# Sliding-window attention and a feed-forward layer on one core: group 1's last additions between the value rows of batch 2, its last block transposed on TensorE, and batch 4's loads and casts ahead of the row scalings of batch 3

## The chip, the cores and the metric

The kernel runs on one core of a Trainium2 chip. The metric is the device time of one execution in microseconds (us). Before the change the median of three runs is 306.37 us (306.21 to 306.56).

## What is computed

Attention with 8 batches, 8 heads, 576 positions and 64 values per head; a position sees itself and the 63 before it. Its output, with the heads side by side, is the input x of a normalised two-layer feed-forward block with a residual:

```
scores = q @ k^T / 8            # masked to 0 <= i - j < 64
attn   = softmax(scores)
x      = attn @ v               # 8 x 576 x 512
xn     = (x - mean) / sqrt(var + 1e-6) * g_ln
out    = x + relu(xn @ w_ch1) @ w_ch2      # 512 -> 2048 -> 512
```

## The kernel before

**Groups.** The first 512 positions of batch g are group g (0 to 7); the last 64 positions of all batches make group 8. While TensorE (PE) runs the feed-forward products of group g, the same loop iteration also runs the attention of batch g+1 in between, and loads and casts batch g+2. A block is 128 of a group's 512 rows, so a group has blocks 0 to 3; "(2,3)" below is batch 2, block 3.

**Units and slots.** The products of a group are a list of 30 units (`mlp_units`). In groups 1 and 2, units 0 to 7 are the first layer for blocks 0 and 1, units 8 to 15 the first layer for blocks 2 and 3 (`l1_half`, L639, tile hph, 8 matmuls each, evacuated with a ReLU by ScalarE (ACT), L644, into hrT). Two PSUM banks ("mm") take turns, so unit n+2 waits for the evacuation of unit n. Units 16 to 29 are the second layer as seven half-size products (L572, banks pA, pB, pC); their operands are sums that VectorE (DVE) makes of hrT (`s_sums`, L546) and of the second weights (`w2_sums`, L833). DVE adds each finished bank into x (`post`, L585; `post_both`, L581), and the rows are stored (L533). Group 3 and later use full-width first-layer units (L498, tile hps), whose first unit reads all four blocks of zT.

Everything else is put between the units by hand: `at(i, f, ...)` appends a step to slot i, which is issued after unit i; slot 30 is after the last unit. Within a slot, steps go in the order in which they were appended. Each engine and each DMA queue works its instructions in that order; waits come from the data and from buffers that are used again.

**The steps of a block.** `s_pe` (L349): scores on PE, into the banks "sc", "xps" or the two banks t0 and t1 ("t"). `s_exp` (L359): two exponentials on ACT. `s_mask` (L369): one multiplication on DVE. `b_pe` (L396): the product with v. `b_rows`: on DVE reciprocal and scaling by rows into x_norm (L412, L416), then mean and variance (L418, L421). `z_step`: three small operations on POOL (GpSimd; L440 to L442, tile rsz), and from batch 3 on the normalised block z there too (L446); for batches 1 and 2 z is made apart, by `z_act` (ACT, L452), `z_dve` (DVE, L461) or `z_pool` (POOL, L457). `zt_step`: transposes z into zT, for batches 0 and 1 by four PE transposes (L475) and a copy by ACT (L478) or DVE (L480), from batch 2 on by a DMA transpose on SP's queue (L471), apart from block 3 of batches 3 and 5.

**The steps of a batch.** `load_qk(b, half)` (L92) and `load_v` (L176): loads on SP's queue; a half is four heads. `cast_qk` (L154) and `cast_v` (L182): POOL. `t_main(b, x, half)`: transposes q (x = 0) or k (x = 1) of four heads into qkT, for batch 2 on PE (L276) with a copy by ACT (L257) or DVE (L259); from batch 3 on q goes by a DMA transpose (L265). `part_vB` (L201, L203): copies by DMA. `load_tail`, `cast_tail`, `t_tail` (L104 to L106, L116 to L118, L298, L307): the same for two batches' rows of group 8. qkT of batch b is the buffer of batch b-2. z has three buffers, so z of (3,3) takes that of (3,0). A PE transpose in group 2 takes bank t0 or t1.

The steps of group 1 are at L1010 to L1074; those of group 2 at L1075 to L1080, the shared part L1081 to L1126, and L1134 to L1152.

Of the kernel before, what the change touches and what calls it, by code (L numbers as in the profile page):

```python
# [10 lines left out]
FP32 = mybir.dt.float32  # L11
FP16 = mybir.dt.float16
AF = mybir.ActivationFunctionType
ALU = mybir.AluOpType
# [4 lines left out]
def kernel(  # L19
# [10 lines left out]
    nc = tc.nc  # L30
    B, H, S, D = q.shape
# [3 lines left out]
    NGRP = B + 1  # L35
# [5 lines left out]
    XZ = 2  # L41
# [9 lines left out]
    p_blk = ctx.enter_context(tc.tile_pool(name="pblk", bufs=3))  # L51
# [28 lines left out]
    x_norm, zT, mvg, zsd, rstd = {}, {}, {}, {}, {}  # L80
# [316 lines left out]
                                 rhs=rhs, start=True, stop=True)  # L397

    def b_rows(g, kb):
        kblk = f"{g}_{kb}"  # L400
        sfx, nb = ("r", 2) if g == NGRP - 1 else ("", None)
        if kb % 2 == 0:
            if (g, kb // 2) not in x_norm:
                for h in ((1, 0) if g // 2 == 2 else (0, 1)):
                    x_norm[(g, h)] = p_xn.tile([128, 2, DM], FP32, tag="xn" + sfx, name=f"xn_{g}_{h}", bufs=nb)
        xv = x_norm[(g, kb // 2)][:, kb % 2, :]
        xn = xv.rearrange("p (h d) -> p h d", h=H)
        tiles = xpss.pop((g, kb))
        n = H // len(tiles)
        rcp = p_blk.tile([128, H], FP32, tag="rcp", name=f"rcp_{kblk}")  # L410
        for i, xps in enumerate(tiles):
            nc.vector.reciprocal(out=rcp[:, n * i:n * i + n], in_=xps[:, :, D])  # L412
        for i, xps in enumerate(tiles):
            rc = rcp[:, n * i:n * i + n]
            rcp_b = bass.AP(tensor=rc.tensor, offset=rc.offset, ap=[rc.ap[0], rc.ap[1], [0, D]])
            nc.vector.tensor_tensor(out=xn[:, n * i:n * i + n], in0=xps[:, :, 0:D], in1=rcp_b, op=ALU.mult)  # L416
        stats = p_blk.tile([128, nc.vector.BN_STATS_DIM], FP32, tag="stats", name=f"stats_{kblk}")
        nc.vector.bn_stats(out=stats, in_=xv)  # L418
        if g not in mvg:
            mvg[g] = p_grp.tile([128, 4, 2], FP32, tag="mvg" + sfx, name=f"mvg_{g}", bufs=1 if sfx else 2)  # L420
        nc.vector.bn_aggr(out=mvg[g][:, kb, :], in_=stats)  # L421
        if g == 0 and kb != 2:
            z_step(g, kb)
# [24 lines left out]
    rsnm = {}  # L448
# [3 lines left out]
        nc.scalar.activation(out=zsd[(g, kb)], in_=x_norm[(g, kb // 2)][:, kb % 2, :], func=AF.Identity,  # L452
                             bias=nm, scale=rs)

    def z_pool(g, kb):
        rs, nm = rsnm[(g, kb)]
        nc.gpsimd.tensor_scalar(out=zsd[(g, kb)], in0=x_norm[(g, kb // 2)][:, kb % 2, :], scalar1=rs, scalar2=nm,  # L457
                                op0=ALU.mult, op1=ALU.add)

    def z_dve(g, kb):  # L460
        nc.vector.tensor_scalar(out=zsd[(g, kb)], in0=x_norm[(g, kb // 2)][:, kb % 2, :],  # L461
                                scalar1=mvg[g][:, kb, 0:1], scalar2=rsnm[(g, kb)][0],
# [2 lines left out]
    def zt_step(g, kb, eng="act"):  # L465
        z = zsd.pop((g, kb))
        if g not in zT:
            sfx = "r" if g == NGRP - 1 else ""
            zT[g] = p_grp.tile([128, NKC, 512], FP16, tag="zT" + sfx, name=f"zT_{g}", bufs=1 if sfx else 2)
        if XZ <= g and not (kb == 3 and g in (3, 5)):  # L470
            nc.sync.dma_start_transpose(out=zT[g][:, :, 128 * kb:128 * kb + 128], in_=z)  # L471
            return
        ztp = t_tile([128, NKC, 128], f"ztp_{g}_{kb}")
        for kc in range(NKC):
            nc.tensor.transpose(out=ztp[:, kc, :], in_=z[:, 128 * kc:128 * (kc + 1)], identity=ident16)  # L475
        dst = zT[g][:, :, 128 * kb:128 * kb + 128]
        if eng == "act":
            nc.scalar.copy(out=dst, in_=ztp)  # L478
        else:
            nc.vector.tensor_copy(out=dst, in_=ztp)  # L480
# [362 lines left out]
    for i in range(8):  # L843
# [8 lines left out]
        out=mask[0:64], in_=mask[0:64], compare_op=ALU.is_gt, fill=0.0,  # L852
# [3 lines left out]
        out=mask[64:128], in_=mask[64:128], compare_op=ALU.is_ge, fill=0.0,  # L856
# [87 lines left out]
    for g in range(NGRP):  # L944
# [7 lines left out]
        def at(i, f, *a):  # L952
            slots[min(i, len(slots) - 1)].append((f, a))

        def first_scores(b, i):
            at(i, s_pe, b, 0)
            at(i, s_pe, b, 1, False, "xps")
            at(i, s_exp, b, 0, 0, 1)
            at(i + 1, s_exp, b, 1, 0, 1)
            at(i + 1, s_mask, b, 0)  # L960
            at(i + 2, s_mask, b, 1)

        b = g + 1
# [46 lines left out]
        if g == 1:  # L1010
            at(0, cast_qk, 2, 0, (0,))
            at(0, after_mask, 1, 3)
            at(0, cast_qk, 2, 0, (1,))
            at(0, cast_qk, 2, 1, (0,))
            at(0, alloc_v, 2)
            at(0, alloc_qkT, 2)
            at(1, t_main, 2, 0, 0)
            at(1, b_pe, 1, 2, "t")
            at(1, b_pe, 1, 3, "sc")
            at(1, b_rows, 1, 2)  # L1020
            at(1, z_step, 1, 2)
            at(1, b_rows, 1, 3)
            at(1, z_step, 1, 3)
            at(1, z_pool, 1, 3)
            at(1, cast_qk, 2, 1, (1,))
            at(2, z_dve, 1, 2)
            at(3, t_main, 2, 1, 0)
            at(4, t_main, 2, 0, 1)
            for c in (0, 2):
                at(4, cast_v, 2, c, c + 2)  # L1030
                at(5, part_vB, 2, c)
            at(5, zt_step, 1, 2)
            at(6, zt_step, 1, 3)
            at(8, t_main, 2, 1, 1)
            for n, i in enumerate((3, 2, 4)):
                at(7, w2_sums, i, 4, 8)
            at(8, s_pe, 2, 0)
            at(8, s_pe, 2, 1, False, "xps")
            at(8, s_exp, 2, 0, 0, 1)
            at(9, s_mask, 2, 0)  # L1040
            at(9, w2_sums, 1, 0, 8)
            at(10, s_exp, 2, 1, 0)
            at(11, s_exp, 2, 1, 1)
            at(12, s_sums, 0, 4, 1, 2)
            at(12, s_mask, 2, 1)
            at(16, s_sums, 4, 8, 1, 2)
            at(20, s_sums, 0, 8, 3)
            at(22, s_sums, 0, 8, 4)
            for j in range(4):
                i = (13, 16, 22, 22)[j]  # L1050
                at(i, b_pe, 2, j, "sc" if j == 3 else "xps")
                if j < 2:
                    at(i, s_mm, 2, j + 2)
                    at(19, s_mask, 2, j + 2)
                i = (13, 17, 25, 25)[j]
                at(i, b_rows, 2, j)
                at(i, z_step, 2, j)
                if j < 3:
                    at((17, 20, 26)[j], z_act, 2, j)
                    at((17, 20, 26)[j], zt_step, 2, j)  # L1060
            at(6, load_qk, 3, 0)
            at(8, load_qk, 3, 1)
            at(10, load_v, 3, 0, 4)
            at(8, alloc_qkT, 3)
            at(8, cast_qk, 3, 0)
            at(14, cast_qk, 3, 1, (0,))
            at(17, cast_qk, 3, 1, (1,))
            at(18, alloc_v, 3)
            at(18, cast_v, 3, 0, 2)
            at(18, cast_v, 3, 2, 4)  # L1070
            at(21, part_vB, 3, 0, 4)
            first_scores(3, 29)
            for i, (x, half) in zip((12, 21, 18, 24), ((0, 0), (1, 0), (0, 1), (1, 1))):
                at(i, t_main, 3, x, half, 0)  # L1074
        if g == 2:  # L1075
            at(2, z_act, 2, 3)
            at(2, zt_step, 2, 3)
            at(3, load_qk, 4, 0)
            at(3, load_qk, 4, 1)
            at(3, load_v, 4, 0, 2)  # L1080
        if g > 1 and b < B:  # L1081
            tail = TAILS.get(g)
            at(2, b_pe, b, 0)
            at(2, b_rows, b, 0)
# [31 lines left out]
            if g + 2 < B:  # L1116
# [2 lines left out]
                at(5, cast_qk, g + 2, 0)  # L1119
                at(5, cast_qk, g + 2, 1, (0,))  # L1120
                at(11, cast_qk, g + 2, 1, (1,))
            for j, i in ((2, 8 if g == 2 else 12), (3, 10 if g == 2 else 19)):
                at(i, b_rows, b, j)
                at(i, z_step, b, j)
            for j in range(4):
                at((4 if g == 2 else 2, 14, 18, {3: 25, 5: 25}.get(b, 23))[j], zt_step, b, j)  # L1126
        for n, i in enumerate(TAILS.get(g, ()) if b >= B else ()):
            ts = (13, 13, 17, 22) if n else (1, 2, 5, 11)
            at(ts[0], s_mm, NGRP - 1, i)
# [3 lines left out]
            at(ts[3], zt_step, NGRP - 1, i)  # L1133
        n = g + 2  # L1134
        if g > 1 and n < B:
            at(3, load_v, n, 2, 4)
            at(17, alloc_v, n)
            at(17, cast_v, n, 0, 2)
            at(17, cast_v, n, 2, 4)
            at(26, part_vB, n, 0, 4)  # L1140
            for i, (x, half) in zip((13, 18, 13, 22) if g == 2 else (13, 17, 13, 21),
                                    ((0, 0), (1, 0), (0, 1), (1, 1))):
                at(i, t_main, n, x, half, 0)
            first_scores(n, 27)
            if n + 1 < B:
                at(40, load_qk, n + 1, 0)
                at(40, load_qk, n + 1, 1)
                at(40, load_v, n + 1, 0, 2)
        if g == 2:
            for c, i in ((0, 12), (4, 16)):  # L1150
                at(i, s_sums, c, c + 4, 1, 2)
                at(i + 2, s_sums, c, c + 4, 3, 4)  # L1152
        if g > 2:
            for i in range(1, 5):
                at(7 + i, s_sums, 0, 4, i)
# [58 lines left out]
```

## Time and profile before

| | |
|---|---|
| Profiled execution | 307.27 us, of which the span (first to last instruction) is 305.5 us |
| Median of the three runs shown | 306.37 us |
| Busy share of the span | PE 95%, weight loads 68%, DVE 71%, ACT 51%, POOL 54% |
| Granted TensorE clock | 0.997 over the span |
| Group 1: first unit starts | 54.02 us |
| Group 2: first unit starts | 90.22 us |
| Group 3: first unit starts | 126.33 us |

Start times are microseconds from the start of the span. A timeline line gives start, duration, engine, source line, operation, what is written and read, how many instructions were merged, and in brackets how long the engine stood idle before it and what ended that. "SPq" is SP's DMA queue: its duration is that of the issue, not of the transfer. PE instructions overlap, so a merged run of eight half-width matmuls shows 1.04 us, while the next can start after 0.87.

### The profile page before, as it was taken

The numbers are of one execution on the slowest core, as the hardware profiler recorded it, in microseconds if no ns is written. First come the engines' busy times: TensorE is split into PE (matmuls) and PEld (weight loads), VectorE is DVE, ScalarE is ACT, GpSimd is POOL, SyncE is SP. The second block draws the span as 40 slices with busy tenths as digits, with TensorE's granted clock in tenths as the row PEclk, the third lists the DMA queues.
The fourth block names the chain that finished last, engine by engine and source line by source line (L and its number), as shares of the span: only waits on it lengthen the run. The fifth ranks groups of instructions, "written<-read, shape, count | busy, mean of one in ns | idle before, by whom it ended". The sixth has DMA issues, their size and how long they took to land.

```text
span 305.5 us, 7808 instructions
## 1 busy us (share of the span) xinstructions
PE 291.7 (95%) x3179; PEld 206.6 (68%) x3179; DVE 217.3 (71%) x412; ACT 154.5 (51%) x260; POOL 165.2 (54%) x244
## 2 busy tenths in 40 slices
PE   8989999979999996999999999999999999999993
PEld 3657545868887885655965597559655864688882
DVE  1881387978895991469956874699568876689982
ACT  3566637567439622785247527852476046405500
POOL 4688877773761589059905962599127607024300
PEclk9999999999999999999999999999999999999998
DMA  8999999949966969799479998993629389003014
GB/s 187 261 384 337 387 266 288 246 158 292 175 150 190 316 130 209 218 309 198 66 212 303 175 186 249 315 157 83 171 66 189 71 158 222 17 19 139 1 36 104
DMA packets 114310, 58.36 MB, mean 191 GB/s; under 512 B 83681, under 2 KB 105249, under 8 KB 114274
## 3 DMA queue, kind: packets, MB, share of 16 engines
q1 hardware_dynamic: 113840, 57.47, 78.2%
q8 instruction: 25, 0.41, 0.6%
q10 hardware_dynamic: 434, 0.40, 0.4%
q14 instruction: 11, 0.09, 0.1%
HBM read 38.80 MB, written 9.44 MB: 158 GB/s over the span
## 4 chain that ended last, share of the span: by engine, by line
PE 72%; DMA 12%; POOL 5%; SPq 3%; DVE 3%; ACT 2%; issue 1%; POOLq 0%; ACTq 0%
PE hps L498 23%; PE pA L572 12%; PE pB L572 8%; PE pC L572 8%; DMA qk<-in_k_dram 6%; PE hph L639 4%; PE xps L396 3%; PE sc L349 3%; DMA qk<-in_q_dram 3%; PE lA L695 2%; PE warm L866 2%; PE tp L276 2%; DMA tk<-in_k_dram 2%; DMA zT<-z 1%; ACT pt L359 1%
## 5 line engine op out<-in xcount | busy, mean ns | idle before, releaser
L498 PE MATMUL hps<-zT,w1g 128*128 128x512 f16 x352 | 80.2, 379 | 0.3 <-DMA zT<-z 0.3
L502 ACT ACTIVATE hrT<-hps 128x512 f16<-128x512 f32 x88 | 52.8, 600 | 37.3 <-PE hps L498 34.2
L498 PEld LDWEIGHTS <-w1g 128*128 128x128 f16 x352 | 33.1, 98 | 38.5 <-issue 1.7
L572 PEld LDWEIGHTS <-sS 128*128 128x128 f16 x512 | 49.4, 98 | 5.7
L359 ACT ACTIVATE pt<-sc 128x512 f16<-128x512 f32 x72 | 39.3, 599 | 21.4 <-PE sc L349 20.8
L440 POOL TENSOR_SCALAR rsz<-mvg 128x1 f32<-128x1 f32 x32 | 10.7, 333 | 65.3 <-DVE mvg L421 55.9
L572 PEld LDWEIGHTS <-hrT 128*128 128x128 f16 x384 | 36.7, 98 | 6.9 <-ACT hrT L502 0.8
L154 POOL CAST qk<-qk 128x1024 f16<-128x1024 f32 x29 | 33.0, 1149 | 13.0 <-DMA qk<-in_q_dram 8.8
L639 PE MATMUL hph<-zT,w1g 128*128 128x256 f16 x320 | 38.0, 273 | 1.1 <-ACT hrT L644 0.6
L369 DVE TENSOR_TENSOR pt<-pt,mask 128x1024 f16<-128x1024 f16 x32 | 23.8, 752 | 19.0 <-ACT pt L359 19.0
L639 PEld LDWEIGHTS <-w1g 128*128 128x128 f16 x320 | 30.4, 98 | 5.8 <-issue 1.6
L572 PE MATMUL pC<-w2s,sS 128*128 128x256 f16 x256 | 30.9, 273 | 0.0
L572 PE MATMUL pA<-wT,sS 128*128 128x256 f16 x256 | 30.9, 273 | 0.0
L257 ACT COPY qkT<-tp 128x1024 f16<-128x1024 f16 (+1 forms) x18 | 17.3, 962 | 26.7 <-PE tp L276 24.9
L644 ACT ACTIVATE hrT<-hph 128x512 f16<-128x512 f32 x40 | 23.9, 600 | 10.7 <-PE hph L639 10.4
L546 DVE TENSOR_TENSOR sS<-hrT 128x1024 f16<-128x1024 f16 (+2 forms) x41 | 26.3, 640 | 3.2 <-ACT hrT L502 2.0
L416 DVE TENSOR_TENSOR xn<-xps,rcp 128x256 f32<-128x256 f32 (+1 forms) x50 | 25.8, 539 | 1.8 <-DMA out_dram<-xn 1.1
L418 DVE BATCH_NORM_STATS2 stats<-xn 128x6 f32<-128x512 f32 x36 | 25.0, 695 | 1.2
L446 POOL TENSOR_SCALAR z<-xn,rsz 128x512 f16<-128x512 f32 x24 | 22.4, 934 | 2.5
L441 POOL TENSOR_TENSOR rsz<-rsz,mhalf 128x1 f32<-128x1 f32 x32 | 20.9, 654 | 2.7
L182 POOL CAST vA<-v 128x1024 f16<-128x1024 f32 (+1 forms) x18 | 16.6, 939 | 5.2 <-DMA v<-in_v_dram 5.0
L396 PEld LDWEIGHTS <-pt 128*64 128x64 f16 x576 | 11.6, 110 | 9.1 <-issue 5.3
(121 smaller groups left out, 419.2 us busy)
## 6 DMA issues: line engine op xcount, KB each, us to landing
qk<-in_q_dram SPq DMA_DIRECT2D x16, 512.0 KB, 6.0
qk<-in_k_dram SPq DMA_DIRECT2D x16, 512.0 KB, 7.4
out_dram<-xn SPq DMA_DIRECT2D x32, 256.0 KB, 3.1
v<-in_v_dram SPq DMA_DIRECT2D x28, 256.0 KB, 6.4
w2s<-in_moe_w_ch_dram SPq DMA_DIRECT2D x9, 512.0 KB, 8.7
w1s<-in_moe_w_ch_dram SPq DMA_DIRECT2D x4, 512.0 KB, 7.3
tk<-in_k_dram SPq DMA_DIRECT2D x8, 256.0 KB, 4.5
tv<-in_v_dram SPq DMA_DIRECT2D x8, 256.0 KB, 5.2
```

The lines of the kernel that those rows point to most:

```text
L154: nc.gpsimd.tensor_copy(out=dst[:, :].rearrange("p (a j) e d -> p a e j d", j=j), in_=t[:, :].rearrange("p (a e j d) -> p a e j d", e=2, j ...
L359: nc.scalar.activation(out=o, in_=i, func=AF.Exp, bias=0.0, scale=scale)
L369: nc.vector.tensor_tensor(out=ptv, in0=ptv, in1=mb, op=ALU.mult)
L416: nc.vector.tensor_tensor(out=xn[:, n * i:n * i + n], in0=xps[:, :, 0:D], in1=rcp_b, op=ALU.mult)
L418: nc.vector.bn_stats(out=stats, in_=xv)
L446: nc.gpsimd.tensor_scalar(out=z, in0=xv, scalar1=rs, scalar2=nm, op0=ALU.mult, op1=ALU.add)
L498: nc.tensor.matmul(out=hps, lhsT=w1g[:, kc, 128 * hc:128 * (hc + 1)], rhs=zT[g][:, kc, :], start=(kc == 0), stop=(kc == NKC - 1),)
L502: nc.scalar.activation(out=hrT[:, hc, :], in_=hps, func=AF.Relu, bias=0.0, scale=1.0)
L546: nc.vector.tensor_tensor(out=o, in0=x, in1=y, op=op)
L572: nc.tensor.matmul(out=o, lhsT=a[:, c, 128 * p:128 * p + 128], rhs=wv[:, c, :], start=(first and (p == 0 or split_c) and c == 0), stop=(c ...
L639: nc.tensor.matmul(out=hps[:, e], lhsT=w1g[:, kc, 128 * hc:128 * (hc + 1)], rhs=zT[g][:, kc, 256 * half:256 * half + 256], start=(kc == 0) ...
L644: nc.scalar.activation(out=hrT[:, 2 * i:2 * i + 2, 256 * half:256 * half + 256], in_=hps, func=AF.Relu, bias=0.0, scale=1.0)
```

## The change

Group 1. z of block (1,3) is made by DVE instead of POOL, and its transpose moves from slot 6 to 7 with its copy on DVE instead of ACT. `w2_sums` moves from slot 7 to 8. The scores of (2,0) and (2,1) move from slot 8 to 7, and the PE transpose of batch 2's k, heads 4 to 7, from slot 8 (ahead of these scores) to slot 10 (behind them). `b_rows` is cut in two; for (2,3) the scaling stays in slot 25, while mean and variance and the POOL operations go to slot 30, behind the group's last two additions into x. The exponentials of (3,1) and both masks of (3,0) and (3,1) move into group 2's first slots.

Group 2. Block (2,3) is transposed on PE in slot 6 with a copy by ACT, not by DMA from slot 2. The loads of q and k of batch 4 move from slot 3 to 0. The steps of batch 3's blocks move one to four slots back, and all four casts of batch 4's q and k go to slot 7, ahead of the POOL steps of blocks (3,1), (3,2) and (3,3); before, the last was in slot 11, behind them. Two `s_sums` move back.

```
     def b_rows(g, kb):
+        b_mult(g, kb)
+        b_stats(g, kb)
...
-        if XZ <= g and not (kb == 3 and g in (3, 5)):
+        if XZ <= g and not (kb == 3 and g in (2, 3, 5)):
             nc.sync.dma_start_transpose(out=zT[g][:, :, 128 * kb:128 * kb + 128], in_=z)
...
-            at(1, z_pool, 1, 3)
...
+            at(4, z_dve, 1, 3)
...
-            at(6, zt_step, 1, 3)
-            at(8, t_main, 2, 1, 1)
+            at(7, zt_step, 1, 3, "dve")
+            at(10, t_main, 2, 1, 1)
             for n, i in enumerate((3, 2, 4)):
-                at(7, w2_sums, i, 4, 8)
-            at(8, s_pe, 2, 0)
-            at(8, s_pe, 2, 1, False, "xps")
+                at(8, w2_sums, i, 4, 8)
+            at(7, s_pe, 2, 0)
+            at(7, s_pe, 2, 1, False, "xps")
...
-                at(i, b_rows, 2, j)
+                at(i, b_mult, 2, j)
+                if j == 3:
+                    i = 30
+                at(i, b_stats, 2, j)
...
-            first_scores(3, 29)
+            at(29, s_pe, 3, 0)
+            at(29, s_pe, 3, 1, False, "xps")
+            at(29, s_exp, 3, 0, 0, 1)
...
         if g == 2:
-            at(2, z_act, 2, 3)
-            at(2, zt_step, 2, 3)
-            at(3, load_qk, 4, 0)
-            at(3, load_qk, 4, 1)
-            at(3, load_v, 4, 0, 2)
-        if g > 1 and b < B:
+            at(0, load_qk, 4, 0)
+            at(0, load_qk, 4, 1)
+            at(0, s_exp, 3, 1, 0)
+            at(0, s_mask, 3, 0)
+            at(1, s_exp, 3, 1, 1)
+            at(2, s_mask, 3, 1)
+            at(3, load_v, 4, 0, 4)
+            at(3, b_pe, 3, 0)
+            at(3, s_pe, 3, 2)
+            at(3, s_pe, 3, 3, False, "t")
+            at(6, zt_step, 2, 3, "act")
+            for i, x in enumerate(((2, 0), (2, 1), (3, 0), (3, 1))):
+                at(3 + i, s_exp, 3, *x)
+            at(4, z_act, 2, 3)
+            at(5, s_mask, 3, 2)
+            at(5, b_rows, 3, 0)
+            at(5, z_step, 3, 0)
+            at(7, s_mask, 3, 3)
+            at(7, alloc_qkT, 4)
+            at(7, after_mask, 3, 3)
+            at(7, cast_qk, 4, 0)
+            at(7, cast_qk, 4, 1)
+            for j in range(1, 4):
+                at(9, b_pe, 3, j, ("xps", "t", "sc")[j - 1])
+                at((9, 10, 12)[j - 1], b_rows, 3, j)
+                at((9, 10, 12)[j - 1], z_step, 3, j)
+            for j, i in enumerate((8, 14, 18, 25)):
+                at(i, zt_step, 3, j)
+        elif g > 1 and b < B:
...
-            for c, i in ((0, 12), (4, 16)):
+            for c, i in ((0, 13), (4, 16)):
                 at(i, s_sums, c, c + 4, 1, 2)
-                at(i + 2, s_sums, c, c + 4, 3, 4)
+                at(18 + c // 2, s_sums, c, c + 4, 3, 4)
```

## The prediction

> **What bounds the kernel now.** I first read the page's busy shares: PE is busy 95% of the span and DVE, the next, 71%. So time falls only where PE stands, and a step on another engine counts only by the PE wait that it makes or ends. The list of PE's waits then names the places:
>
> ```profile
> engine line waited for: us in total, times, longest us
> PE tp L276 <- POOL qk L154: 2.8, 1, 2.8
> ...
> PE sc L349 <- DVE qkT L259: 1.1, 1, 1.1
> ...
> PE hph L639 <- ACT hrT L644: 0.6, 1, 0.6
> PE ztp L475 <- POOL z L457: 0.6, 1, 0.6
> ...
> PE hph L639 <- DVE xn L581: 0.4, 1, 0.4
> PE hps L498 <- DMA zT<-z: 0.3, 1, 0.3
> ```
>
> All six lie in groups 1 and 2, where the change is made. The timeline gives their places. Group 1:
>
> ```profile
> 62.11 1.21 POOL L457 TENSOR_SCALAR z<-xn,rsz 128x512 f16<-128x512 f32 x1
> ...
> 63.37 0.40 PE L475 MATMUL ztp<-ident,z 128*128 128x128 f16 x4 [0.55 <-POOL z L457]
> ...
> 66.00 1.23 DVE L259 COPY qkT<-tp 128x1024 f16<-128x1024 f16 x1 [0.71 <-PE tp L276]
> ...
> 67.28 0.52 PE L349 MATMUL sc<-qkT,qkT 64*128 64x64 f16 x24 [1.10 <-DVE qkT L259]
> ```
>
> PE waits for POOL's z of (1,3), then for the copy of k's second half, which a quarter of the scores' matmuls came ahead of. Then SP's queue in group 2:
>
> ```profile
> 93.06 2.00 SPq L533 DMA_DIRECT2D out_dram<-xn  x4
> 95.74 1.23 SPq L471 DMA_TRANSPOSE zT<-z  x1
> 97.03 0.57 SPq L92 DMA_DIRECT2D qk<-in_q_dram  x1
> ...
> 99.93 8.98 SPq L176 DMA_DIRECT2D v<-in_v_dram  x4
> 109.02 2.48 SPq L471 DMA_TRANSPOSE zT<-z  x1
> ...
> 120.89 2.64 SPq L471 DMA_TRANSPOSE zT<-z  x2
> ```
>
> From 97.03 to 123.53 no gap in it is over 0.12 us: loads of batch 4, (3,0)'s transpose, six tail loads (111.54 to 116.59), two transposes of q, and last the transposes of (3,1) and (3,2). The last is issued at 122.31 and lands 3.97 later, at 126.28; group 3 starts at 126.33. The chain of work that ended last runs through this queue. And PE, from the same stretch:
>
> ```profile
> 113.63 1.04 PE L572 MATMUL pA<-wT,sS 128*128 128x256 f16 x8
> 117.43 0.62 PE L276 MATMUL tp<-ident,qk 128*128 128x128 f16 x8 [2.76 <-POOL qk L154]
> ...
> 126.33 1.90 PE L498 MATMUL hps<-zT,w1g 128*128 128x512 f16 x8 [0.34 <-DMA zT<-z]
> ```
>
> Two limits thus stand 0.3 us apart at group 3's start: PE with its 2.9 us hole, and SP's queue. Taking the hole alone would bring 0.3.
>
> **Group 1, slots 6 to 16.** From unit 6's end (61.78 + 0.87 = 62.65) to the value product in slot 16 (75.83) are 13.2 us. PE's work in it: ten units at 0.875 (two start 1.75 apart), 0.22 and 0.45 for two transposes, 0.57 for 32 scores, 0.72 for slot 13: 10.7. So 2.5 are waits: 0.7 for z, 1.2 for k, the rest in four pieces.
>
> After the change z of (1,3) needs the root on POOL (61.63) and DVE behind its copy of qkT (62.08); by the other DVE row (0.52) it is ready at 62.6, ahead of PE. Its copy by DVE (0.43) runs beside the 0.57 of scores, which leaves 0.15 of wait. The scores no longer wait for k: they are issued ahead of its second transpose. That also means that heads 4 to 7 of blocks (2,0) and (2,1) are scored with what this buffer holds from batch 0; the wait goes because the order goes. POOL loses 1.21, so batch 2's casts come 1.2 earlier.
>
> What is late next: DVE. Moved behind the copy, `w2_sums` runs from 64.4; its three rows take 0.68, 1.15 and 1.41 (3.2), a mask 0.7, the fourth sum 1.22, k's copy 1.22: k is there at 70.8. PE reaches slot 13 at 70.3, does 0.35 of value product, and waits 0.2 for k. Then 1.4 of `s_sums`, mask 0.7, reciprocal and scaling 0.95: the bank for slot 16 is free at 73.8, and PE is there at 74.0. ACT costs two waits of 0.15. Sum: 2.5 − 0.7 of waits left: **1.8 gained**. The ends: the three sums at 0.68 each save 1.2 on DVE, at 1.41 each cost 1.0. The first shortens a 0.2 wait, the second makes 0.8 of new wait: 1.0 to 2.0.
>
> The Trainium skill (SBUF — State Buffer, "Who interferes with whom") says that a DVE instruction with two SBUF inputs contends with a GpSimd one that reads SBUF; this speaks against the move, which puts the sums beside the casts of v. The rows of 0.68 and 1.41 fit it, and by it alone group 1 gains 1.0.
>
> The rest of group 1 follows: its later PE waits are 0.2 each, and DVE there waits for PE (0.7, 0.6). Group 2 starts at 90.22 − 1.8 = 88.4.
>
> **Group 2, units 0 to 9.** I count in the old clock and subtract 1.8 at the end. Mean and variance moved behind `post_both` free its bank about 0.85 earlier (90.8 for 91.64), so unit 1 does not wait. Of four exponentials ahead of the first ReLU two go behind it: unit 2 starts at 92.4 for 93.35. But ACT now has, from 90.77 to unit 9, eight exponentials and eight ReLUs at 0.48 to 0.5 start to start (four exponentials took 2.04), z 0.7 and one new copy 0.5. In the order written, ACT ends the first exponential of (3,3) at 99.0; only then is bank t0 free for the new PE transpose of (2,3), and PE, there at 97.8, waits 1.2. The copy lands at 100.1, unit 8 follows, and unit 9 waits for unit 7's ReLU until 101.1. With the value products now behind unit 9, unit 10 starts at 102.9, before at 102.6. **Cost 0.3.** Ends: ACT's first waits do not shorten (+0.9), or the t0 wait falls away (−1.2).
>
> **POOL.** The same operations in another order. q and k of batch 4 are cast in slot 7, from about 100.3 (new clock, behind (3,0)'s z) to 105; the last was at 116.33. PE needs them at 109 and 113, so the 2.9 hole closes. Behind them stand z of (3,1) to (3,3): 8.6 with all waits before (107.80 to 116.39), so z of (3,3) at about 113.6. One new wait: its buffer is (3,0)'s, whose transpose now stands behind the tail loads and lands near 115; PE transposes it at 116. Casts of v (2.03) and tail (2.9) end near 121, used at 118.5 and later. These fit, with under 1 us of cover.
>
> PE alone would reach group 3 at 126.33 − 1.8 + 0.3 − 2.9 − 0.3 (zT) − 0.3 (scores of (4,0), 0.89 for 0.57) = **121.3**.
>
> **SP's queue.** (2,3)'s transpose leaves it, and loads start directly behind the stores: 95.1 for 97.03, 1.9 earlier, and 1.8 more by group 1: 3.7. What follows is the same set (tail loads only change places with (3,0)'s transpose), 25.3 us from first load to the last transpose's issue. So that transpose lands at 126.28 − 3.7 = **122.6**, and group 3 starts there: PE waits 1.3. Bounds for the queue: a DMA transpose of q took 2.76 and 1.24, of z 1.22 to 2.48, the dear ones directly behind loads. If one dear place goes, 1.3 is saved and PE's 121.3 binds. If the data path is the limit (four stores of 256 KB were moving until 97, and v's issues of one size take 0.79 to 4.30), the 1.9 is lost.
>
> The Trainium skill (Perfetto Trace Analysis, "What 'DMA-bound' means") calls a solid issuing track descriptor generation, not data movement; by it the queue moves rigidly with its first entry, 3.7. The unequal v issues speak for waiting on data in part.
>
> **Sum.** 126.33 − 122.6 = 3.7 at group 3's start. Behind that PE has no listed wait, loads and transposes follow the group's end, so it stays: 307.27 − 3.7 = 303.6 for the profiled execution, which lies 0.9 above the median; on the median 306.37 − 3.7 = **302.7**.
>
> **Rivals.**
> 1. Forecast: SP's queue sets group 3's start. Gain 3.2 to 4.3, so 302.1 to 303.2. Chance 0.45.
> 2. PE sets it, the queue having drained faster: gain 5.0, 301.4. For it: dear transposes came directly behind loads. Against: the bytes are the same. Chance 0.2.
> 3. The early loads gain nothing, since stores and 256-byte rows of v fill the data path; group 1's gain alone remains: 306.37 − 1.8 = 304.6. For it: v's issue took 8.7 and 9.0 in both groups. Against: the DMA share was 0.55 and 0.42 in 90 to 94. Chance 0.25.
> 4. Nothing remains: ACT's queue in group 2's first units gives back what group 1 won. 306.4. It needs ACT 5 us longer. Chance 0.04.
> 5. Slower: POOL stands at the cast of k's second half, and three z steps, v and the tail stand behind it, where before they were ahead. If that half lands at X, z of (3,3) is there at X + 1.04 + 8.6, and PE needs 5.2 from its transpose to group 3: X + 14.8 passes 126.3 from X = 111.5. I expect it near 103.4 (issued 95.0, landing 8.4 as before). Two microseconds past the point give 308.4. Chance 0.06.
>
> Faster by over 0.2% (0.6 us, about what a measurement here can tell from no change): cases 1 to 3, 0.90; within it, case 4, 0.04; slower 0.06. The range takes in 1 to 3: 301.3 to 304.8.
>
> **What would show it.** Right: no PE wait at L475 and L276; the first load of batch 4 near 93.3; PE waiting about 1.2 for t0 in unit 6's place; a PE wait at L498 for zT of about 1.3, with group 3 at 122.6. Wrong: group 3 without that wait (case 2); the last transpose of z issued at 120 or later (case 3); a POOL wait for k over 3 us (case 5); group 2 starting later than 89.5 (DVE's sums). What would upset all is a PE wait of several us that has no row above.

## The result: 302.0 us, and the profile after

The changed kernel takes 302.0 us (median of four runs, 301.72 to 302.41); the kernel before, measured beside it, takes 306.47 (306.21 to 307.1). The ratio is 0.9852, with a 95% interval of 0.9833 to 0.9872: **4.5 us less**, where 3.7 were forecast. The profiled execution took 301.72 us with a span of 300.0. The two profiled executions differ by 5.55, about 1 more than the medians: the one of before lay 0.8 above its median, the one of the changed kernel 0.3 below its own.

The stages by the start of PE's first matmul in the two traces; the first row is a time, the others are lengths, in us:

| Stage | before | after | difference |
|---|---|---|---|
| Group 1, start | 54.02 | 53.50 | −0.52 |
| Group 1, length | 36.20 | 34.20 | −2.00 |
| Group 2, units 0 to 9 | 12.37 | 12.85 | +0.48 |
| Group 2, unit 10 to group 3's start | 23.74 | 20.50 | −3.24 |
| From group 3 (126.33, now 121.05) to the end | 179.17 | 178.95 | −0.22 |

The first row is no part of the change, which touches nothing ahead of group 1: two experiments below that hold before's code up to there start group 1 at 53.57 and 53.70. It belongs to the one execution of before that was profiled.

The list of PE's waits in the changed kernel, in the same form as that of before:

```profile
...
PE ztp L478 <- ACT pt L359: 1.1, 1, 1.1
PE xps L396 <- ACT pt L359: 0.8, 3, 0.3
...
PE tp L276 <- POOL qk L154: 0.5, 1, 0.5
PE ztp L478 <- POOL z L454: 0.3, 1, 0.3
PE hph L642 <- ACT hrT L647: 0.2, 1, 0.2
```

The wait of 2.8 for POOL's cast and that of 1.1 for the copy of k are gone, and so is the one for zT (the row of 0.5 for POOL's cast stands at 14.31 us, far ahead of the change). One of 1.1 is new: the PE transpose of (2,3) waits for the exponential that frees bank t0. PE's timeline in the changed kernel shows where these rows stand:

```profile
62.94 0.39 PE L478 MATMUL ztp<-ident,z 128*128 128x128 f16 x4
63.26 0.64 PE L349 MATMUL sc<-qkT,qkT 64*128 64x64 f16 x32
...
96.64 0.38 PE L478 MATMUL ztp<-ident,z 128*128 128x128 f16 x4 [1.10 <-ACT pt L359]
...
112.46 0.61 PE L276 MATMUL tp<-ident,qk 128*128 128x128 f16 x8
...
115.94 0.40 PE L478 MATMUL ztp<-ident,z 128*128 128x128 f16 x4 [0.25 <-POOL z L454]
...
121.05 2.78 PE L501 MATMUL hps<-zT,w1g 128*128 128x512 f16 x12
```

Group 1's scores now run as one piece of 32 (before: 8, a wait, 24). The transpose of k's second half at 112.46 starts without a wait, where before PE stood for 2.76. Group 3 starts at 121.05 with no wait for zT beside it. As the prediction said, heads 4 to 7 of blocks (2,0) and (2,1) are scored with what the buffer holds from batch 0, so these scores are not those of q and k of batch 2; this holds for all kernels below that have group 1 as the change has it (`g1_only`, `a_ref`, `a_lastcast`, `a_lastwarm`, `a_t0`, `a_tail`, `a_dma`). Those that put k's transpose ahead of the scores (`a_order`, `a_order2`, `a_best`, `a_best3`) use batch 2's own k.

SP's queue in the changed kernel:

```profile
92.15 0.56 SPq L92 DMA_DIRECT2D qk<-in_q_dram  x1
...
94.79 8.68 SPq L176 DMA_DIRECT2D v<-in_v_dram  x4
...
110.71 1.69 SPq L474 DMA_TRANSPOSE zT<-z  x1
...
115.20 2.56 SPq L474 DMA_TRANSPOSE zT<-z  x2
```

The first load of batch 4 is issued at 92.15 (before: 97.03). All following times count from the span's start, so 0.52 of any difference to before comes from ahead of group 1. The transpose of (3,0) stands behind the tail loads now, is issued at 110.71 and lands 4.2 later, near 115. The last transpose is issued at 116.5 and lands 4.4 later, at 120.9, which is 0.15 ahead of group 3. POOL, from the same trace:

```profile
99.95 3.98 POOL L154 CAST qk<-qk 128x1024 f16<-128x1024 f32 x4
...
115.12 0.77 POOL L454 TENSOR_SCALAR z<-xn,rsz 128x512 f16<-128x512 f32 x1 [2.79 <-DMA zT<-z]
```

All four casts now run in one stretch, 8.5 us ahead of PE's use of the last. The z of (3,3) waits 2.79 for the buffer of (3,0), whose transpose has just landed; that leaves PE the wait of 0.25 at 115.94. So three things stand within 0.3 us of one another at group 3's start: PE's own work, POOL's z of (3,3), and the queue's last transpose.

### The profile page after: what moved, and what is told of

It reads as the page before. It is cut to its first block, busy times and chain, and to the rows that moved or that the text cites. A ratio compares the mean times of both kernels' runs of the same rounds, so it can differ in the third digit from the quotient of the medians.

```text
span 300.0 us, 7816 instructions
## 1 busy us (share of the span) xinstructions
PE 290.4 (97%) x3183; PEld 206.2 (69%) x3183; DVE 219.3 (73%) x414; ACT 154.4 (51%) x260; POOL 164.9 (55%) x243
## 4 chain that ended last, share of the span: by engine, by line
PE 85%; DMA 4%; SPq 4%; POOL 2%; issue 1%; ACT 1%; DVE 1%; POOLq 0%; ACTq 0%
PE hps L501 26%; PE pA L575 12%; PE hph L642 10%; PE pB L575 9%; PE pC L575 8%; PE xps L396 4%; PE ch L659 4%; PE sc L349 3%; DMA w1s<-in_moe_w_ch_dram 3%; PE lA L698 2%; PE tp L276 2%; SPq L176 2%; DMA zT<-z 1%; SPq L87 1%; PE lC L698 1%
## 5 line engine op out<-in xcount | busy, mean ns | idle before, releaser
L369 DVE TENSOR_TENSOR pt<-pt,mask 128x1024 f16<-128x1024 f16 x32 | 24.6, 775 | 20.1 <-ACT pt L359 20.1
L549 DVE TENSOR_TENSOR sS<-hrT 128x1024 f16<-128x1024 f16 (+2 forms) x41 | 27.3, 665 | 1.8 <-ACT hrT L505 1.8
```

The costliest lines, as they stand in the source:

```text
L369: nc.vector.tensor_tensor(out=ptv, in0=ptv, in1=mb, op=ALU.mult)
L549: nc.vector.tensor_tensor(out=o, in0=x, in1=y, op=op)
```

## The experiments

**The theories.** The prediction's own is that of two limits: PE's hole and SP's queue had to move together. By it group 1 brings about 1.8 by itself, and group 2's part brings its share only because casts and loads move at once. Against it stands the late cast: it was all of the cost, and moved alone it brings most of the gain. On group 1 there are two. Either its gain is that the scores no longer need k, so that it can't be had with batch 2's own k; or what costs is the series of transpose, copy and scores, whatever their order. On what is left of PE's waits, those for t0 and for (3,0)'s buffer may still cost time that comes free when they go.

The kernels were run in three comparisons, each on one chip with the kernel before beside them (medians 305.68, 305.92 and 306.01). A ratio is to the kernel before of the same comparison; it is not the quotient of the medians, so that a gain by the ratio can differ by some tenths of a us from one by the medians.

### The cast alone: b_casts

```
-                at(11, cast_qk, g + 2, 1, (1,))
+                at(5 if g == 2 else 11, cast_qk, g + 2, 1, (1,))
```

> The kernel before, with one edit: the cast of batch 4's k, second half, goes from slot 11 to slot 5 of group 2, ahead of the POOL steps of (3,1) to (3,3). Theory of two limits side by side: PE's 2.9 us hole closes, but group 3 still starts with the landing of (3,2)'s transpose, so PE's wait at L498 grows from 0.3 to about 3 and the time falls by 0.1 to 0.3 only: 306.1 to 306.3. Rival, the hole is the loss: 2.9 less, 303.5.

Measured: 306.01 us (304.45 to 308.3), ratio 1.002 (0.9991 to 1.0049). **No gain**, so the late cast was not all of it. The profiled execution was its fastest of twelve. PE's timeline in it:

```profile
120.22 0.53 PE L349 MATMUL sc<-qkT,qkT 64*128 64x64 f16 x24 [0.69 <-DMA qkT<-qk]
...
123.47 0.82 PE L498 MATMUL hps<-zT,w1g 128*128 128x512 f16 x3 [0.20 <-DMA zT<-z]
```

With the hole gone PE meets the queue twice: at the transposes of q and at zT. The second wait is 0.2 and not near 3, because in this execution the queue took 26.9 us from its first load (96.53) to the landing of its last zT (123.4), where before's profiled execution took 29.25 for the same transfers. Read alone, this execution would show a gain: group 2 takes 33.70 in it (89.77 to 123.47), against 36.11 in before's trace. The medians show none, so a trace of one execution doesn't stand for the typical one here. That the slower executions (four of twelve took 307.5 to 308.3, at a mean clock of 0.990 to 0.994) held a longer wait at zT is possible, but none of them was profiled.

### Group 1 alone: g1_only

The kernel before, with the group-1 slots 1 to 10 of the change and nothing else of it:

```
-            at(1, z_pool, 1, 3)
...
+            at(4, z_dve, 1, 3)
...
-            at(6, zt_step, 1, 3)
-            at(8, t_main, 2, 1, 1)
+            at(7, zt_step, 1, 3, "dve")
+            at(10, t_main, 2, 1, 1)
...
```

> The kernel before, with group 1's edits in slots 1 to 10 alone (z of (1,3) on DVE, its transpose in slot 7 with a DVE copy, the second weights' sums in slot 8, the scores of (2,0) and (2,1) in slot 7 ahead of the transpose of k, which goes to slot 10; as in the changed kernel, heads 4 to 7 of these two blocks are scored with what the buffer of k held before). Theory: group 1 is 1.8 to 1.9 shorter, and everything behind it, SP's queue included, moves with it: 304.5. Rival, SP's queue in group 2 does not follow group 1's end, so little arrives: 305.9 to 306.4.

Measured: 303.9 us (302.99 to 305.77), ratio 0.9947 (0.9922 to 0.9971): 1.6 less than before by the ratio, 1.8 by the medians. Group 1 runs from 53.70 to 87.88, 34.18, against 36.20 before and 34.20 in the changed kernel: the slots 1 to 10 are the whole of group 1's gain. In its trace the hole for POOL's cast is still there, but it is 1.73 and not 2.76: POOL waited 2.48 for the loads of q and k of batch 4 ahead of its casts, where in before's trace it waited 3.71. So the hole is no limit of PE's own; it follows the loads in SP's queue. Group 3 starts behind waits of 0.5 for the transposes of q and 0.4 for zT. Five of its twelve executions ran at a mean clock of 0.993 or 0.994 and took 305.05 to 305.77; the other seven, at 0.997 or more, took 302.99 to 304.22.

### The order of scores and k: a_order and a_order2

Both keep the changed kernel and put k's second transpose ahead of the scores again. `a_order` only moves it:

```
-            at(10, t_main, 2, 1, 1)
+            at(7, t_main, 2, 1, 1)
```

> The changed kernel with the transpose of batch 2's k, heads 4 to 7, put back ahead of the scores that read it, all in slot 7, copied by DVE as before. The scores then use batch 2's own k. Theory: PE waits again for that copy; scores end near 65.5 for 63.85 with 0.45 of it moved work, so 1.1 to 1.2 more than the changed kernel: 303.1 to 303.2. Rival, the wait went by the other moves of group 1 and not by the order: 302.0 to 302.2.

`a_order2` moves it, lets ACT make the copy instead of DVE, and puts the scores one slot later, so that unit 8 runs while the copy is made:

```
-            at(10, t_main, 2, 1, 1)
+            at(7, t_main, 2, 1, 1, 0)
...
-            at(7, s_pe, 2, 0)
-            at(7, s_pe, 2, 1, False, "xps")
+            at(8, s_pe, 2, 0)
+            at(8, s_pe, 2, 1, False, "xps")
```

> The changed kernel with the transpose of batch 2's k, heads 4 to 7, in slot 7, copied by ACT (which is idle from 63.7 to 64.9 there), and the scores of (2,0) and (2,1) behind it in slot 8. The scores use batch 2's own k. Theory: unit 8 covers the copy, so the right order costs 0 to 0.3 over the changed kernel: 302.0 to 302.3. Rival, the order costs its 1.1 wherever it is put, since ACT's exponentials and DVE's mask come a unit later: 303.1.

Measured: `a_order` 303.05 us (302.94 to 304.49), ratio 0.9919 (0.9895 to 0.9942); `a_order2` 301.97 (301.49 to 302.71), ratio 0.9876 (0.9854 to 0.9898). PE's timeline, first of `a_order`:

```profile
65.13 0.52 PE L349 MATMUL sc<-qkT,qkT 64*128 64x64 f16 x24 [1.10 <-DVE qkT L259]
```

then of `a_order2`:

```profile
63.23 0.61 PE L276 MATMUL tp<-ident,qk 128*128 128x128 f16 x8
63.91 1.05 PE L642 MATMUL hph<-zT,w1g 128*128 128x256 f16 x8
64.89 0.64 PE L349 MATMUL sc<-qkT,qkT 64*128 64x64 f16 x32
```

The wait of before comes back to the hundredth (1.10), and costs its length: `a_order` takes 1.08 more than `a_order2` by the medians, 1.3 by the ratios. With a unit between transpose and scores, and the copy on an idle engine, it vanishes; which of the two it takes was not separated. So what costs is the copy in series, not the order. The changed kernel did not run in this comparison; its ratio of 0.9852 (0.9833 to 0.9872) and the 0.9876 of `a_order2` overlap within their intervals, so batch 2's own k costs nothing that these runs can tell, 0.7 us at the centres.

### The changed kernel again: a_ref

> The changed kernel itself, as the measure for the three others of this call (heads 4 to 7 of (2,0) and (2,1) scored with what the buffer of k held before, here and in the three others). Both theories: 302.0, group 3 at 121.0 to 121.2 in the profile.

Measured: 301.72 us (301.12 to 302.57), ratio 0.9856 (0.9832 to 0.988); group 3 at 121.05. `a_lastcast`, `a_t0` and `a_tail` ran beside it and are read against it.

### The cast back behind the z steps: a_lastcast, and a_lastwarm

```
-            at(7, cast_qk, 4, 1)
+            at(7, cast_qk, 4, 1, (0,))
+            at(13, cast_qk, 4, 1, (1,))
```

> The changed kernel with the cast of batch 4's k, second half, put back behind the POOL steps of (3,1) to (3,3), slot 13. Theory: z of (3,3) still stands until the transpose of (3,0) has landed (114.95), so the cast ends at about 116.9 and PE, there at 112.5, waits 4.4: 4.2 more than the changed kernel, 306.2; this one step undone gives nearly the whole gain back. Rival, the gain of group 2 came with the earlier loads and SP's queue: 302.0 to 302.5.

Measured: 307.66 us (306.49 to 309.46), ratio 1.0057 (1.0033 to 1.0081): 5.9 more than `a_ref`. PE's timeline in `a_lastcast`:

```profile
116.53 1.04 PE L276 MATMUL tp<-ident,qk 128*128 128x128 f16 x8 [3.90 <-POOL qk L154]
...
119.07 3.38 PE L575 MATMUL pC<-w2s,sS 128*128 128x256 f16 x16
```

The cast stands behind the z of (3,3), and that waits 4.24 for (3,0)'s buffer, so PE waits 3.9 for the cast, where 4.4 were expected. Yet group 3 comes at 127.35, 6.3 later than in the changed kernel. The second row shows where the rest is: 16 such matmuls took 1.91 in the changed kernel, 3.38 here. The table by windows of `a_lastcast` (start and end, length, then busy time with instructions in brackets of PE, PEld, DVE, ACT and POOL, the granted PE clock, DMA share, GB/s) gives the reason:

```profile
111.82:115.23 3.41, 0.81 (x8) 0.49 (x5) 1.02 (x2) 0.00 (x0) 0.50 (x1) 1.00 1.25 193
115.23:118.65 3.42, 2.12 (x15) 1.75 (x16) 0.00 (x0) 1.01 (x1) 3.42 (x6) 0.50 0.59 124
118.65:122.06 3.41, 3.41 (x18) 2.41 (x17) 0.69 (x1) 0.00 (x0) 2.37 (x3) 0.50 0.54 137
122.06:125.47 3.41, 3.41 (x62) 2.94 (x61) 1.71 (x2) 1.27 (x3) 0.00 (x0) 1.00 0.02 5
```

The granted clock falls to 0.50 at 115.23, 2.6 us into PE's idle stretch, and stays there until 122.06; all eleven executions have a mean clock of 0.988 to 0.993. To tell the clock from the wait, `a_lastwarm` adds 14 matmuls on zeros in slot 22, ahead of the wait; their bank is read by nothing:

```
+            at(22, fill, 14)
```

> The kernel with the last cast behind the z steps (slot 13), plus 14 matmuls of 512 columns of zeros into a free bank in PE's hole in slot 22, ahead of the transpose that waits; they feed nothing. (Heads 4 to 7 of (2,0) and (2,1) are scored with what the buffer of k held before.) Its trace showed a granted clock of 0.50 from 116 to 122 behind the 3.9 us hole. Theory: 2.1 to 2.3 us of that kernel's loss are the clock and not the wait; with the hole filled to under 1 us the clock stays at 1.0 and the time falls from 307.7 to about 305.5, though PE does 3 us more work. Rival, the clock drop is a mark of the waiting and costs nothing beyond it: 307.7 or more.

Measured: 305.85 us (305.1 to 307.78), ratio 0.9991 (0.9969 to 1.0013). PE's timeline in `a_lastwarm`:

```profile
112.67 3.19 PE L877 MATMUL fill<-wfill 128*128 128x512 f16 x14
117.13 0.62 PE L276 MATMUL tp<-ident,qk 128*128 128x128 f16 x8 [1.27 <-POOL qk L154]
```

PE does 3.2 us more work, waits only 1.27, its clock stays at 1.00 in all windows from 112 to 124, and the kernel is 1.8 us faster than `a_lastcast` (by the ratios, each against the kernel before of its comparison, 0.0066 or 2.0 us). So the wait and the clock are two costs: some 4 us (305.85 against the 301.72 of `a_ref`, by the ratios 4.1) and some 2 us.

### The wait for t0 taken away: a_t0

```
+            at(2, z_dve, 2, 3)
...
-            at(3, s_pe, 3, 3, False, "t")
-            at(6, zt_step, 2, 3, "act")
+            at(4, zt_step, 2, 3, "dve")
+            at(5, s_pe, 3, 3, False, "t")
...
-            at(4, z_act, 2, 3)
```

> The changed kernel with PE's 1.1 us wait for bank t0 taken away: z of (2,3) made by DVE in slot 2, its PE transpose in slot 4 with a DVE copy, ahead of the scores of (3,3), which go to slot 5. Theory: PE gains 1.1 there and loses it again, standing at the transpose of (3,3) for POOL's z (0.25 now, 1.3 then) and for zT, which lands at 120.9: 0 to 0.3 less, 301.7 to 302.0. Rival, PE's waits add up: 1.1 to 1.4 less, 300.6 to 300.9.

Measured: 302.02 us (301.08 to 304.24), ratio 0.9873 (0.9838 to 0.9908): no gain. PE's timeline in `a_t0`:

```profile
93.41 0.39 PE L478 MATMUL ztp<-ident,z 128*128 128x128 f16 x4
...
116.66 0.40 PE L478 MATMUL ztp<-ident,z 128*128 128x128 f16 x4 [2.00 <-POOL z L454]
```

The wait of 1.1 is gone at 93.41, and comes back as 2.0 at 116.66, because POOL's z of (3,3) waits 3.6 for the transpose of (3,0). The wait for t0 cost nothing that these runs can tell: a wait ahead of a limit that doesn't move is worth nothing.

### The tail loads behind (3,0)'s transpose: a_tail

```
-                at(4, load_tail, i)
+                at(8 if g == 2 else 4, load_tail, i)
```

> The changed kernel with the six tail loads behind the transpose of (3,0) in SP's queue (slot 8 for 4). Theory: that transpose lands 5 to 6 us earlier and POOL's 2.8 us wait for its buffer goes, but PE's wait behind it is only 0.25, and the last transpose of z lands when it did (120.9): 0 to 0.25 less, 301.75 to 302.0. Rival, POOL's wait stands on the path that ends last: 1 to 2.5 less.

Measured: 301.43 us (300.98 to 302.5), ratio 0.985 (0.9823 to 0.9876), 0.3 below `a_ref`, which these runs don't tell from none. POOL's wait of 2.8 is gone, and PE's of 0.25; but the last transpose of z is issued at 116.8 and lands at 120.8, and group 3 starts at 120.90. PE's weight load there waits 0.22 for zT. With POOL out of the way the queue is the limit, 0.15 earlier.

### The transpose of (2,3) back on the queue: a_dma

```
-        if XZ <= g and not (kb == 3 and g in (2, 3, 5)):
+        if XZ <= g and not (kb == 3 and g in (3, 5)):
...
-            at(0, load_qk, 4, 0)
-            at(0, load_qk, 4, 1)
...
+            at(2, z_act, 2, 3)
+            at(3, zt_step, 2, 3)
+            at(3, load_qk, 4, 0)
+            at(3, load_qk, 4, 1)
...
```

> The changed kernel with (2,3) transposed by DMA again: z by ACT and the DMA transpose in group 2's slots 2 and 3, ahead of the loads of batch 4 (also in slot 3), as in the queue before. (Heads 4 to 7 of (2,0) and (2,1) are scored with what the buffer of k held before.) Theory: PE's 1.1 us wait for t0 and its transpose go, but the loads start 2 us later, and the last transpose of z lands at about 122.9: 1.5 to 2 more than the changed kernel, 303.3 to 303.8. Rival, the queue has slack and only PE's own work counts: 1.1 to 1.3 less, 300.5.

Measured: 304.55 us (302.36 to 305.88), ratio 0.9934 (0.9904 to 0.9963). The edit takes back two things at once, the transpose on PE and the loads in slot 0. The first load is issued at 94.04, 1.9 later than in the changed kernel. PE's timeline in `a_dma`:

```profile
117.66 0.58 PE L478 MATMUL ztp<-ident,z 128*128 128x128 f16 x4 [2.96 <-POOL z L454]
118.04 3.43 PE L575 MATMUL pA<-wT,sS 128*128 128x256 f16 x16
```

The later loads did not reach PE through the last transposes, as was expected, but through z of (3,3), which waited 3.3 for (3,0)'s buffer; and behind the idle of 2.96 the clock stood at 0.50 from 117.73 to 121.14 (the 16 matmuls of 1.91 took 3.43). Seven of the twelve executions ran at a mean clock of 0.992 to 0.994, with a median of 305.06; the five at 0.998 or more have a median of 303.06. So (2,3) on PE with the earlier loads is worth about 1.3 us where the clock holds (303.06 against the 301.72 of `a_ref`, in another comparison), and 2 more where it falls.

### Put together: a_best and a_best3

`a_best` is the changed kernel with `a_order2`, `a_t0` and `a_tail` in one.

> The changed kernel with three edits: batch 2's k transposed in slot 7 ahead of the scores (slot 8), which use batch 2's own k; PE's wait for t0 taken away (z of (2,3) by DVE in slot 2, its transpose in slot 4, scores of (3,3) in slot 5); and the tail loads behind the transpose of (3,0). Theory: two of the three limits at group 3's start go, the third stays, the landing of (3,2)'s transpose near 120.9: 0 to 0.4 less than the changed kernel, 301.4 to 301.8, with a PE wait for zT of about 1 at L501. Rival, SP's queue is not a limit: 1.1 to 1.4 less, 300.4.

Measured: 300.89 us (300.37 to 301.41), ratio 0.982 (0.9791 to 0.9849), against the kernel before in the same comparison 5.1 less by the medians, and 0.5 below the least that was expected. Group 3 starts at 120.10; PE's matmuls list no wait for t0, for z or for zT, but the weight load at group 3's start waits 0.31 for zT, and the last transpose lands at 120.0: the queue is still the limit, 0.9 earlier than expected. Against the changed kernel it is 0.8 less (301.72 for `a_ref`, in another comparison on another chip): its six executions end at 301.41, and of the ten of the changed kernel one (301.12) lies below that, but the two intervals of the ratio overlap. Faster than before is shown; faster than the change is likely.

`a_best3` goes on from there: the transposes of q ahead of the tail loads, and (3,2) transposed on PE in slot 20, so that only one transpose stands behind the tail loads:

```
-        if XZ <= g and not (kb == 3 and g in (2, 3, 5)):
+        if XZ <= g and not (kb == 3 and g in (2, 3, 5)) and (g, kb) != (3, 2):
...
-            for j, i in enumerate((8, 14, 18, 25)):
+            for j, i in enumerate((8, 14, 20, 25)):
...
-            for i, (x, half) in zip((13, 18, 13, 22) if g == 2 else (13, 17, 13, 21),
+            for i, (x, half) in zip((8, 18, 8, 22) if g == 2 else (13, 17, 13, 21),
...
-                at(8 if g == 2 else 4, load_tail, i)
+                at(9 if g == 2 else 4, load_tail, i)
...
```

> As the kernel with three edits, and SP's queue shortened and reordered as well: batch 4's q transposes in slot 8, directly behind that of (3,0), the tail loads behind them in slot 9, and (3,2) transposed on PE in slot 20 with a copy by ACT. The scores use batch 2's own k. Theory: all three limits go; PE does 0.22 more and reaches group 3 at about 119.8: 1.0 to 1.3 less than the changed kernel, 300.4 to 300.7. Rival, the tail casts on POOL now wait for their loads and hold PE at the tail's transposes: 301.5 or more.

Measured: 301.79 us (301.38 to 302.55), ratio 0.9854 (0.9824 to 0.9883). A miss: the queue's last transpose of z lands at 118.8, but PE has 0.23 more work and waits 0.52 for POOL's z of (3,2); group 3 starts at 120.67. PE's own work and POOL are the limit now.

## Why the prediction came out right, and which term was off

The time lies in the range, but the step that the forecast named did not happen. Its first case was that SP's queue sets group 3's start and PE waits 1.3 for zT. That wait did not come; group 3 without it was the prediction's own sign for its second case, PE as the limit. That 302.0 lies only 0.7 from the 302.7 of the first case is in part luck: the two cases stood 1.3 apart, and the queue's last landing came 0.15 ahead of PE's own limit. Forecast times below count from before's trace; 0.52 is taken off where it says so, since the profiled execution of the changed kernel started group 1 that much earlier.

- **Two limits at group 3's start** ("taking the hole alone would bring 0.3"): right by the time. `b_casts` takes the hole alone and brings nothing that can be measured. The trace of before was a costlier execution than most, so that the distance of 0.3 was read in an execution whose queue took 29.25; in the one of `b_casts` PE met the queue again at 26.9. What the prediction did not say is that the hole itself follows the queue: it was 2.76 and 1.73 in two executions with the same steps in group 2, as POOL waited 3.71 and 2.48 for the loads. So the two limits are not independent: the loads feed both.
- **Group 1, 1.8** (1.0 to 2.0): measured 2.0 in the traces of the changed kernel and of `g1_only`, and 1.6 to 1.8 in the time of `g1_only`. The term of DVE's sums was a little dear: they took 0.68, 1.41 and 0.69, 2.8 instead of 3.2, so k's copy ended at 69.5 and not 70.3 (70.8 less 0.52), and the wait of 0.2 for it did not come. The reason given for the scores (the order) was too narrow: `a_order2` has the old order at the same time. The rule of the Trainium skill (SBUF — State Buffer, "Who interferes with whom"), by which alone the gain would be 1.0, fits the two sums that ran beside a cast of v: the first took 0.68, but the cast beside it 1.56 (1.04 in before); the second took 1.41. The third ran alone. By the time it decided nothing here.
- **Group 2, units 0 to 9, cost 0.3**: measured 0.48, with a wait for t0 of 1.10 for 1.2 forecast, and unit 10 at 100.55 for 100.6 (101.1 less 0.52). Right, though `a_t0` shows that this cost never reached the end.
- **POOL, "under 1 us of cover"**: right, and less than that. Casts ended at 103.9 (104.5 forecast, less 0.52). z of (3,3) was there for PE at 115.94 (115.5 forecast, less 0.52), behind exactly the buffer that the prediction named, and the cover was gone: PE waited 0.25. `a_lastcast`, `a_t0` and `a_dma` all lose time through this one wait. Rival 5 (slower: POOL stands at the cast of k, with all else behind it) did not come: k's second half landed at 102.7 (102.9 forecast, less 0.52), 8.8 ahead of its point of 111.5, and the casts ran without a wait for the loads. `a_lastcast` shows the price of POOL reaching that cast late: 5.9.
- **PE alone, 121.3**: with the 0.52 by which this execution started group 1 earlier, the forecast is 120.8; measured 121.05, which holds the 0.25 of wait for POOL's z.
- **SP's queue, 3.7: the mis-sized term.** The last zT was to land at 122.6 with PE waiting 1.3; it landed at 120.9 and PE did not wait. Of 5.4 in all, 0.52 came ahead of group 1, 2.0 (for 1.8) from group 1, 2.36 (for 1.9) from what left the queue ahead of the loads, the 0.45 more being that the transpose of (2,2) was issued in 1.63 instead of 2.08, and 0.5 from the stretch between first load and last landing, 28.75 for 29.25. Inside that stretch the prediction's dear places did get cheaper, (3,0)'s transpose 1.69 for 2.48 and those of q 2.60 for 4.11 together; but the six tail loads, now ahead of them, took 7.1 for 5.05 from the first issue to the end of the last, so most of it was only moved. So the saving of 1.9 was not lost (rival 3), and PE's own limit and the queue's came out within 0.2 of each other. The time lies between the two cases: 302.0, where rival 1 began at 302.1 and rival 2 stood at 301.4. The rule of the Trainium skill (Perfetto Trace Analysis, "What 'DMA-bound' means"), from which the prediction took that the queue moves rigidly with its first entry, is not borne out in that reading: the first entry moved by 4.9 and the last landing by 5.4, and the same transfers took 26.9 in `b_casts`.
- **What the sum left out: the granted clock.** In the hole of before PE waited 2.76 us, at a clock of 1.00 in the profiled execution. But of the 62 executions of before in the three comparisons, 11 have a mean clock of 0.993 or 0.994, with a median of 307.2 us, against 305.6 for the other 51. None of the ten executions of the changed kernel falls under 0.996. On the mean that is 11/62 × 1.6, about 0.3 us, an estimate; for the four executions of before behind the 306.47 no clock is on record. That it is the hole that brings these executions about was not profiled, only its like in `a_dma`.

What stays open: why the queue's length differs between executions for the same transfers, what group 2's part would bring without group 1's (it was not run), and by how much `a_best` beats the changed kernel.

## What to carry to other kernels

Where two limits meet at one point, move both at once, and look for the resource that couples them: here a block's transpose in SP's queue freed the buffer that POOL's last step needed, and three experiments (`a_lastcast`, `a_t0`, `a_dma`) lost time through that one buffer. Cover a copy between two steps of the bound engine with a unit of its other work and an idle engine, before changing the order of what needs it. A wait of the bound engine ahead of the next limit is no gain to take; ask first where the time would come back, as the 1.1 at t0 came back as 2.0.

## What the runs showed of the hardware

**The clock is granted in steps of 3.41 us, and an idle stretch of less than 3 us can halve it.** Within the kernels the traces show it at 1.00 for 293.55 us (the changed kernel), 296.96 (before), 112.64 and 180.91 (`a_dma`), 109.23 and 184.32 (`a_lastcast`), and at 0.50 for 3.41 (`a_dma`) and 6.83 (`a_lastcast`). Each is a whole number of times 3.413: 86, 87, 33, 53, 32, 54, 1 and 2. So it changed only at edges that lie 3.413 apart. Cut at these edges, the stretch ahead of the fall held 0.81 us of PE's work in `a_lastcast` (111.82 to 115.23, shown above) and 0.45 in `a_dma` (114.32 to 117.73). In before's trace an edge falls into the hole of 2.76 and leaves more work on both sides, 2.35 and 1.70, and the clock holds (columns as in the table above):

```profile
112.31:115.72 3.41, 2.35 (x22) 1.85 (x19) 1.58 (x3) 0.00 (x0) 2.84 (x7) 1.00 0.72 160
115.72:119.13 3.41, 1.70 (x20) 1.58 (x21) 0.17 (x1) 1.01 (x1) 3.41 (x4) 1.00 1.36 194
119.13:122.54 3.41, 3.41 (x35) 2.92 (x32) 1.21 (x2) 0.59 (x1) 2.88 (x5) 1.00 1.22 207
```

So where a hole lies against the edges can decide whether the clock falls. This fits that executions of one kernel differ, and that before's 11 slow-clock executions lost about 1.6 us: one step of 3.41 at 0.50 is worth 1.7, an estimate. That these 11 have their fall at the hole is not shown. By PE's timeline the fall cost 1.6 in `a_dma` (6.74 from the transpose that waited to group 3, against 5.11 in the changed kernel) and 2.7 in `a_lastcast` (10.82, against 8.14 in `a_lastwarm`); 14 matmuls that filled the idle stretch took it away. The Trainium skill (TensorE: Matmul & The Clock Gate, Part 1) says that the clock falls after an idle window of about 3.4 us, and that this window runs freely. The length of the steps agrees with it; that the window must be idle throughout does not, with 0.81 us of work in the one ahead of the fall in `a_lastcast`.

**A DMA queue's length is not fixed by its transfers.** From the first load of batch 4 to the last landing of zT it took 29.25 us in before, 28.75 in the changed kernel and 26.9 in `b_casts`, with the same transfers (in the changed kernel (3,0)'s transpose changes places with the tail loads).
